# Sine features of k for two of eight batches, made by GpSimd in four forms of instruction

## The chip, the cores and the metric

The kernel runs on one core of one Trainium2 chip. The metric is the device time of the whole program in microseconds. A core has TensorE (PE, matmuls), VectorE (DVE), ScalarE (ACT), GpSimd (POOL) and SyncE (SP, which here only issues DMAs). Each engine takes its instructions in the order in which the program lists them and waits where an operand is not ready.

## The reference

q, k and v have 8 batches of 8 heads, 576 positions and 64 dimensions, in float32. The first half is a linear attention with position weights, the second a gated two-layer network over its output.

```python
theta = np.pi / 2.0 * pos / S
phi(x) = concat([relu(x) * cos(theta), relu(x) * sin(theta)])     # 64 -> 128 features
kv  = einsum('bhsf,bhsd->bhfd', phi(k), v);   z = phi(k).sum(over s)
num = einsum('bhsf,bhfd->bhsd', phi(q), kv)
den = einsum('bhsf,bhf->bhs', phi(q), z) + 1e-6
x   = (num / den), as 4608 rows of 512
h   = x @ w_in                                                   # 512 -> 2048
out = (h * cos(h)) @ w_out                                       # 2048 -> 512
```

Both cosine and sine are positive on the positions used, so relu(x) times the weight equals relu of the product.

## The kernel before

**Tiles.** A batch is laid out as five tiles t = 0 to 4 of 128 rows: each partition holds 4 or 5 positions, and which partitions hold five alternates between even and odd batches. Raw k, q and v come by DMA into one float32 buffer each (tiles km, qm, vm; two DMAs per batch and tensor, L427 and L430). There is one buffer per tensor, so the load of the next batch's k waits until the last feature of this batch's k has been read.

**Features.** `prep` (L443) makes one feature of one tile: 128 partitions by 8 heads by 64 values, g = 0 for cosine and g = 1 for sine, so ten steps per batch for k and ten for q. The weight is a scalar per partition (`CS[:, b % 2, g, t:t+1]`). ACT does it in one activation (Relu with a scale, L452), DVE in one tensor_scalar (maximum with 0, then the product, L453). The result goes as float16 into `kp` or `qp`, both parts of the tile KQ, in blocks of 64 values that lie 128 apart. `cast_v` (L457) casts v to float16, on DVE, ACT or GpSimd (L466 to L468).

**Users.** `kv` (L471) multiplies all k features of a batch with v on TensorE (L479) into the PSUM bank ATT. It needs all ten features and all casts of v. q features are transposed by DMA on the SP queue (`q_dma`, L520), `num` (L542) multiplies them with kv, DVE divides (L568), x is transposed by DMA on SP (`x_dma`, L599) and goes to the two layers: layer 1 in L677 (plain) and L780 (a scheme with seven products of halves, for which DVE makes sums XS of x at L738 and WS of w_in at L717), the gate cos(h) * h by ACT (L609, L802) and DVE (L614, L808), layer 2 in L948 with sums at L926 and L979. TensorE works at layer 1 of one batch and layer 2 of the batch before while the attention of the next batch is prepared.

**What sets the order.** Nothing runs in the order in which the source lists it. Every step is entered in a planner (`Plan`, L129) with its engine or its possible engines, a cost for each, what it reads and writes, and a position in the list KEYS. `Plan.forward` (L183) is a list scheduler: it keeps a clock for each engine, and gives the next step by the smallest key among those that are ready within a small patience. Where a step has several engines, the one that would finish first takes it. Steps marked `port` on DVE and GpSimd are not planned at the same time. Loads become available at their key less 8 us. The program then lists the steps by planned start, which fixes each engine's queue. `either` (L410) enters a step with a choice of engines: cost on DVE is 0.42 us and on ACT 0.62 us for one feature.

In the planner's order for this kernel the ten sine features of k of batches 4 and 5 stand on these engines: batch 4, t = 0 and 2 on DVE and t = 1, 3 and 4 on ACT; batch 5, t = 1 and 3 on DVE and t = 0, 2 and 4 on ACT.

Of the kernel before, what the change touches and what calls it, by code (L numbers as in the profile page):

```python
# [11 lines left out]
ALU = mybir.AluOpType  # L12
# [280 lines left out]
def kernel(  # L293
# [9 lines left out]
    nc = tc.nc  # L303
    B, H, S, D = q.shape
    Dm, Dff = moe_w_in.shape
    P = 128
# [24 lines left out]
    pool = ctx.enter_context(tc.tile_pool(name="pool", bufs=1))  # L331
# [3 lines left out]
    def sb(name, shape, dt=F16):  # L335
        return pool.tile(shape, dt, name=name)
# [73 lines left out]
    def either(due, cost, fn, rd, wr):  # L410

        lat = {"DVE": 0.13, "ACT": 0.15, "POOL": 0.15}
        pl.add([(e, cost[e], cost[e] + lat[e], fn[e]) for e in cost], 0, 0, due, None, rd, wr, port=True)
# [25 lines left out]
    def hk(nm, hs=range(H)):  # L439
        return [((nm, h), n) for h in hs for n in range(2)]  # L440


    def prep(b, nm, t, g, eng, due, hs=slice(0, H), after=()):  # L443
        dst = (kp if nm == "k" else qp)
        out_, in_ = dst[:, t, hs, g, :], raw[nm][:, hs, t, :]
        sc = CS[:, b % 2, g, t:t + 1]
        heads = range(H)[hs]
        rd = hk(nm, heads) + ["CS", *after]
        wr = [(nm + "p", t, g, h) for h in heads]
        f = len(heads) / H  # L450
        cost = {"DVE": 0.09 + 0.33 * f, "ACT": 0.12 + 0.5 * f}
        fn = {"ACT": lambda: nc.scalar.activation(out=out_, in_=in_, func=AF.Relu, scale=sc),  # L452
              "DVE": lambda: nc.vector.tensor_scalar(  # L453
                  out=out_, in0=in_, scalar1=0.0, scalar2=sc, op0=ALU.max, op1=ALU.mult)}
        either(due, {e: c for e, c in cost.items() if eng in (e, "")}, fn, rd, wr)

    def cast_v(b, t, eng, due, hs=slice(0, H), nt=1):  # L457
# [233 lines left out]
    for g in WS:  # L691
        if g < OWN:
            t = sb(f"WS{g}", [P, 3, CH2, GW])
            WS[g].update({n: t[:, n - 2] for n in (2, 3, 4)})
        else:
            for n in (2, 3, 4):
                t = qT[n // 4].rearrange("p h s -> p (h s)").rearrange("p (i c f) -> p i c f", i=2, c=CH2)
# [367 lines left out]
    def first_attention():  # L1065
        for i, nm in enumerate("qkv"):
            dve(0.53, i - 9, lambda nm=nm: nc.vector.memset(raw[nm][:, :, NT, :], 0.0), [],
                [((nm, h), 0) for h in range(H)])
        warm(14, 6.5)
        for nm in ORDER0:  # L1070
            load(0, nm, 0, HALVES if nm == ORDER0[2] else (slice(0, H),))
        weights()
        for t in range(NT):
            prep(0, "q", t, 0, "DVE", t)
            prep(0, "q", t, 1, "DVE" if t == 1 else "ACT", t)
            q_pe(0, t, *BANKS[t], "ACT" if t % 2 else "DVE", t)
        warm(16, 3.45, rd=[("TR", 0)])
        for t in range(NT + 1):
            prep(0, "k", t, 0, "DVE", 4)
            prep(0, "k", t, 1, "DVE" if t == 2 else "ACT", 4)  # L1080
        for hb in range(2):
            for t in range(NT + 1):
                cast_v(0, t, "ACT" if t % 2 else "DVE", 5 + hb, HALVES[hb])
        kv(0, 7, BANKS2)
        for t in range(NT):
            num(0, t, 8 + t, PAIRS0[t % 2])
            if FILL[t]:
                warm(FILL[t], 0.2157 * FILL[t], M1[1],
                     [(("ATT", "M2")[t % 2], 1)], [("M1", 1), ("fill", t)])
            x_pe(0, t, t, *BANKS[3 - t % 2], "ACT", 8 + t, [("fill", t)])  # L1090
# [108 lines left out]
```

## Time and profile before

| what | value |
|---|---|
| median of the runs shown | 285.25 us (283.92 and 286.57) |
| the profiled execution's own time | 284.34 us |
| its span, first to last instruction | 282.3 us |
| granted TensorE clock | 0.993 |
| PE, DVE, ACT, POOL busy | 270.5, 249.2, 218.0, 19.2 us |
| DVE features of k (L453) | 25, mean 482 ns |
| ACT features of k (L452) | 55, median 712 ns |
| GpSimd casts of v, 128x1024 | 9, mean 1088 ns |
| features of k of batch 4 | 91.3 to 104.5 us |
| matmuls of k and v of batch 4, of batch 5 | 108.4, 132.7 us |

The page gives busy time of each engine; the chain of work that ended last follows the releases back from the last instruction; the groups give, for a line and an operation, the output and input tiles, the shapes, the count, the busy time in us, the mean of one in ns, and the idle time of the engine before them with what ended it. In the time order, each line is the start in us, the length in us, the engine, the line, the operation and the tiles, and "xcount" where several neighbours are merged; idle time of the engine before it stands in brackets with its releaser. SPq lines are the issue of a DMA on SP's queue, not its transfer.

### The profile page before, as it was taken

The numbers are of one execution on the slowest core, as the hardware profiler recorded it, in microseconds if no ns is written. First come the engines' busy times: TensorE is split into PE (matmuls) and PEld (weight loads), VectorE is DVE, ScalarE is ACT, GpSimd is POOL, SyncE is SP. The second block draws the span as 40 slices with busy tenths as digits, with TensorE's granted clock in tenths as the row PEclk, the third lists the DMA queues.
The fourth block names the chain that finished last, engine by engine and source line by source line (L and its number), as shares of the span: only waits on it lengthen the run. The fifth ranks groups of instructions, "written<-read, shape, count | busy, mean of one in ns | idle before, by whom it ended". The sixth has DMA issues, their size and how long they took to land.

```text
span 282.3 us, 6870 instructions
## 1 busy us (share of the span) xinstructions
PE 270.5 (96%) x2715; PEld 219.1 (78%) x2715; DVE 249.2 (88%) x443; ACT 218.0 (77%) x396; POOL 19.2 (7%) x32
## 2 busy tenths in 40 slices
PE   7799988999989999999999999999999999999994
PEld 2668956678967667779787988898788888888883
DVE  2877796999999989998999999999999999997952
ACT  2856698896899998599899999996676675877420
POOL 1440020010000010003003000210000000000000
PEclk9799999999999999999999999999999999999999
DMA  6999999969979999997999899988013100300124
GB/s 204 312 200 222 298 291 267 320 133 285 311 231 235 211 229 293 241 310 161 308 234 268 167 275 270 240 117 251 3 37 116 57 2 0 151 0 2 74 77 149
DMA packets 77599, 53.30 MB, mean 189 GB/s; under 512 B 46080, under 2 KB 75264, under 8 KB 77568
## 3 DMA queue, kind: packets, MB, share of 16 engines
q1 hardware_dynamic: 72608, 48.12, 66.7%
q0 software_dynamic: 4224, 4.19, 9.5%
q10 hardware_dynamic: 736, 0.57, 0.6%
q8 instruction: 21, 0.34, 0.5%
q14 instruction: 10, 0.08, 0.1%
HBM read 36.74 MB, written 9.44 MB: 164 GB/s over the span
## 4 chain that ended last, share of the span: by engine, by line
PE 85%; DVE 5%; DMA 4%; ACT 3%; issue 1%; DVEq 0%
PE M L948 32%; PE M L780 15%; PE M L637 10%; PE M L677 7%; PE TR L780 6%; PE M L880 5%; PE ATT L542 3%; DMA xT<-x 2%; PE ATT L479 2%; DMA qm<-in_q_dram 2%; PE M L509 2%; PE ATT L1022 1%; PE TR L677 1%; DVE x L568 1%; ACT xT L593 1%; ACT KQ L452 1%
## 5 line engine op out<-in xcount | busy, mean ns | idle before, releaser
L609 ACT ACTIVATE ch<-M 128x512 f32<-128x512 f32 x90 | 53.3, 597 | 14.4 <-PE M L637 6.9
L614 DVE TENSOR_TENSOR gT<-M,ch 128x512 f16<-128x512 f32 x84 | 56.7, 685 | 5.0 <-ACT ch L609 4.6
L948 PEld LDWEIGHTS <-gT 128*128 128x128 f16 x560 | 54.0, 98 | 7.6 <-DVE gT L926 0.5
L948 PE MATMUL M<-w_out_sb,gT 128*128 128x256 f16 x448 | 55.9, 273 | 0.0
L452 ACT ACTIVATE KQ<-km,CS 128x512 f16<-128x512 f32 x55 | 37.2, 715 | 0.2 <-DMA km<-in_k_dram 0.2
L452 ACT ACTIVATE KQ<-qm,CS 128x512 f16<-128x512 f32 x47 | 32.3, 721 | 4.5 <-DMA qm<-in_q_dram 4.5
L780 PEld LDWEIGHTS <-w_in_sb 128*128 128x128 f16 x320 | 30.8, 98 | 4.3 <-issue 0.2
L948 PE MATMUL M<-T,S 128*128 128x256 f16 x256 | 32.4, 273 | 0.0
L637 PE MATMUL M<-xT,w_in_sb 128*128 128x256 f16 x256 | 30.2, 273 | 0.1
L677 PE MATMUL M<-xT,w_in_sb 128*128 128x512 f16 x112 | 27.6, 379 | 0.8 <-ACT xT L593 0.8
L948 PEld LDWEIGHTS <-S 128*128 128x128 f16 x256 | 24.7, 98 | 4.0 <-issue 0.2
L637 PEld LDWEIGHTS <-w_in_sb 128*128 128x128 f16 x256 | 24.5, 98 | 3.5 <-issue 0.4
L568 DVE TENSOR_TENSOR x<-ATT,rec 128x512 f16<-128x512 f32 x32 | 22.1, 692 | 2.3
L959 ACT ACTIVATE ost<-M 128x512 f32<-128x512 f32 x24 | 14.1, 593 | 12.1 <-PE M L948 9.3
L780 PEld LDWEIGHTS <-WS 128*128 128x128 f16 x216 | 20.5, 98 | 3.3 <-issue 0.5
L677 PEld LDWEIGHTS <-w_in_sb 128*128 128x128 f16 x128 | 12.2, 98 | 10.8 <-issue 0.9
L453 DVE TENSOR_SCALAR KQ<-qm,CS 128x512 f16<-128x512 f32 x33 | 15.4, 498 | 5.1 <-DMA qm<-in_q_dram 5.1
L468 POOL CAST V<-vm 128x1024 f16<-128x1024 f32 (+1 forms) x11 | 10.7, 1004 | 134.9 <-PE M L948 46.0
L542 PEld LDWEIGHTS <-qT 128*128 128x128 f16 x320 | 15.3, 98 | 4.6 <-issue 1.8
L926 DVE TENSOR_TENSOR S<-gT 128x2048 f16<-128x2048 f16 (+1 forms) x16 | 17.4, 1085 | 0.2
L808 DVE TENSOR_TENSOR gT<-Z,ch 128x1024 f16<-128x1024 f32 x13 | 15.9, 1221 | 0.7 <-ACT ch L802 0.4
L542 PE MATMUL ATT<-kvz,qT 128*128 128x65 f16 x288 | 15.7, 194 | 0.6 <-DVE x L568 0.5
(135 smaller groups left out, 461.3 us busy)
## 6 DMA issues: line engine op xcount, KB each, us to landing
out_dram<-ost SPq DMA_DIRECT2D x33, 256.0 KB, 3.0
qm<-in_q_dram SPq DMA_DIRECT2D x8, 640.0 KB, 5.9
km<-in_k_dram SPq DMA_DIRECT2D x8, 640.0 KB, 5.6
qm<-in_q_dram SPq DMA_DIRECT2D x8, 512.0 KB, 6.2
km<-in_k_dram SPq DMA_DIRECT2D x8, 512.0 KB, 5.7
vm<-in_v_dram SPq DMA_DIRECT2D x6, 640.0 KB, 7.2
vm<-in_v_dram SPq DMA_DIRECT2D x6, 512.0 KB, 6.5
w_in_sb<-in_moe_w_in_dram POOLq DMA_DIRECT2D x4, 512.0 KB, 8.9
```

What stands on the lines that cost most here:

```text
L452: fn = {"ACT": lambda: nc.scalar.activation(out=out_, in_=in_, func=AF.Relu, scale=sc), "DVE": lambda: nc.vector.tensor_scalar(out=out_, i ...
L453: "DVE": lambda: nc.vector.tensor_scalar(out=out_, in0=in_, scalar1=0.0, scalar2=sc, op0=ALU.max, op1=ALU.mult)}
L542: nc.tensor.matmul(bank[hb][:, hh * D1:(hh + 1) * D1], lhsT=a[:, h, :], rhs=z[:, h, :], start=(i == 0), stop=(i == len(parts) - 1))
L568: nc.vector.tensor_tensor(out=split(x16[n][:, hs, :], k), in0=A[:, :, :, 0:D], in1=split(rec[n][:, hs], k).unsqueeze(3).broadcast_to((P, k ...
L609: act(0.5, due, lambda: nc.scalar.activation(out=ch[c], in_=bank, func=AF.Sin, bias=math.pi / 2.0, scale=1.0), [key], [("ch", c)])
L614: dve(0.61, due, lambda: nc.vector.tensor_tensor(out=dst, in0=a, in1=b, op=ALU.mult), [key, ("ch", c), *rd], dkeys)
L637: nc.tensor.matmul(M1[m][:, jj * 2 * P:(jj + 1) * 2 * P], lhsT=w_in_sb[:, cc, j * P:(j + 1) * P], rhs=X[:, cc, ts], start=(cc == 0), stop= ...
L677: nc.tensor.matmul(M, lhsT=w_in_sb[:, cc, j * P:(j + 1) * P], rhs=X[:, cc, :], start=(cc == 0), stop=(cc == NCT - 1))
L780: nc.tensor.matmul(bank[0][:, j * TH:(j + 1) * TH], lhsT=a(cc, j), rhs=b[:, cc, :], start=(first and j == 0 and cc == 0), stop=(last and j ...
L808: dve(1.14, due, lambda: nc.vector.tensor_tensor(out=g4, in0=four(uz), in1=four(cc2), op=ALU.mult), zk + ck, [("g", gi(c), h * JH + j, t) ...
L926: dve(0.07 + 1.07 / NG, due, lambda: nc.vector.tensor_tensor(out=out_[:, sl], in0=a[:, sl], in1=b[:, sl], op=op), rd, wr, port=True)
L948: nc.tensor.matmul(bank[0][:, tt * MH:(tt + 1) * MH], lhsT=a[:, j, tt * P:(tt + 1) * P], rhs=b[:, j, :], start=(first and (apart or tt == ...
```

## The change

The five sine features of k (g = 1) of batches 4 and 5 get GpSimd as their only engine. The planner is told 1.2 us for t = 0 to 3 and 2.0 us for t = 4. The forms differ by t: for t = 0 and 1 one tensor_scalar, maximum with 0 and then the product with the weight; for t = 2 one tensor_scalar with the two in the other order; for t = 3 a two-input product with the weight broadcast along the row, and then a tensor_scalar in place for the maximum; for t = 4 a tensor_scalar for the product, and then one in place for the maximum. The values computed are the same. No other step is edited; KEYS is unchanged, and the planner makes its order anew with the new costs and engines.

```diff
@@ -452,6 +452,21 @@
         fn = {"ACT": lambda: nc.scalar.activation(out=out_, in_=in_, func=AF.Relu, scale=sc),
               "DVE": lambda: nc.vector.tensor_scalar(
                   out=out_, in0=in_, scalar1=0.0, scalar2=sc, op0=ALU.max, op1=ALU.mult)}
+        if b in (4, 5) and nm == "k" and g == 1:
+            def pool():
+                q = nc.gpsimd
+                if t < 2:
+                    q.tensor_scalar(out=out_, in0=in_, scalar1=0.0, scalar2=sc, op0=ALU.max, op1=ALU.mult)
+                elif t == 2:
+                    q.tensor_scalar(out=out_, in0=in_, scalar1=sc, scalar2=0.0, op0=ALU.mult, op1=ALU.max)
+                elif t == 3:
+                    q.tensor_tensor(out=out_, in0=in_, in1=sc.unsqueeze(2).broadcast_to((P, H, D)), op=ALU.mult)
+                    q.tensor_scalar(out=out_, in0=out_, scalar1=0.0, scalar2=None, op0=ALU.max)
+                else:
+                    q.tensor_scalar(out=out_, in0=in_, scalar1=sc, scalar2=None, op0=ALU.mult)
+                    q.tensor_scalar(out=out_, in0=out_, scalar1=0.0, scalar2=None, op0=ALU.max)
+            cost, fn = {"POOL": 1.2 if t < 4 else 2.0}, {"POOL": pool}
+            eng = ""
         either(due, {e: c for e, c in cost.items() if eng in (e, "")}, fn, rd, wr)
```

## The prediction

> **What bounds the kernel now.** I read the busy shares first, then the chain that ended last, then the time order from 85 to 135 us, where batches 4 and 5 are prepared.
>
> ```profile
> span 282.3 us, 6870 instructions
> PE 270.5 (96%) x2715; PEld 219.1 (78%) x2715; DVE 249.2 (88%) x443; ACT 218.0 (77%) x396; POOL 19.2 (7%) x32
> PE 85%; DVE 5%; DMA 4%; ACT 3%; issue 1%; DVEq 0%
> ```
>
> TensorE works 96% of the span and holds 85% of the chain; GpSimd is nearly empty. By stretches, PE is busy 13.10 of 13.10 us between 91.3 and 104.4, and 10.70 of 10.70 between 117.7 and 128.4, the two windows in which k of batches 4 and 5 becomes features. Its idle time from 85 to 135 us is two entries: 0.30 us until DVE's XS at L738, and 0.53 us until DVE's x at L568. So relieving ACT or DVE here can give back at most about 0.83 us, 0.3% of the run. A loss has no such limit, because PE takes its instructions in order.
>
> The time order shows how much room there is:
>
> ```profile
> 91.29 1.32 ACT L452 ACTIVATE KQ<-km,CS 128x512 f16<-128x512 f32 x2
> ...
> 103.80 0.71 ACT L452 ACTIVATE KQ<-km,CS 128x512 f16<-128x512 f32 x1
> 104.45 2.05 POOL L468 CAST V<-vm 128x1024 f16<-128x1024 f32 x2 [46.02 <-PE M L948]
> 104.54 0.76 SPq L427 DMA_DIRECT2D km<-in_k_dram  x1
> 108.39 1.37 PE L479 MATMUL ATT<-V,KQ 128*128 128x65 f16 x40
> ...
> 128.40 2.25 POOL L468 CAST V<-vm 128x1024 f16<-128x1024 f32 x2 [21.89 <-DMA vm<-in_v_dram]
> 132.67 1.37 PE L479 MATMUL ATT<-V,KQ 128*128 128x65 f16 x40
> ```
>
> k of batch 4 is read from 91.29 on. Its last feature ends at 104.51; the two casts of v end at 106.50; the matmuls that use both (L479) start at 108.39. Batch 5: the second half of its k load is issued at 111.99 and lands about 5.7 us later (the median of k loads), so at 117.7; casts at 128.40; matmuls at 132.67. The next k load (SP, 104.54) was issued right after the last feature, since raw k has one buffer.
>
> **The change, part by part.** *Removed.* Per batch, five of the ten features. By the planner's order for the kernel before, the ten steps concerned stand as six on ACT and four on DVE. On ACT two of them back to back take 1.32 us, so one is 0.61 us of the queue: 6 x 0.61 = 3.7 us. On DVE one takes 0.48 us and the next instruction starts 0.40 us after it (92.09 to 92.49): 4 x 0.40 = 1.6 us. All of it lies beside a PE without idle time, so I count the gain as nothing; 0.83 us is its upper end.
>
> *Added.* Seven GpSimd instructions per batch: one each for t = 0, 1 and 2 (two operations, one input), two for t = 3 (a two-input product, then an in-place maximum), two for t = 4 (a product, then an in-place maximum). No row shows one of them. The nearest rows are casts:
>
> ```profile
> L468 POOL CAST V<-vm 128x1024 f16<-128x1024 f32 x9 | 9.7, 1088 | 134.9 <-PE M L948 46.0 <-DMA vm<-in_v_dram 40.6 <-PE M L677 26.9
> L468 POOL CAST V<-vm 128x512 f16<-128x512 f32 x2 | 1.2, 625 | 0.0
> L1052 POOL CAST qm<-w_in_sb 2x1 f32<-2x1 f16 x1 | 0.2, 176 | 0.0
> ```
>
> 512 elements cost 0.625 us; almost none cost 0.18. One pass over 512 is therefore 0.45 us. Lower end: every instruction costs one pass, 7 x 0.625 = 4.4 us, plus 0.3 us twice for an in-place instruction that waits for the one before it (the row for that is the 0.31 us between GpSimd's hold at 10.89 and its first load): 5.0 us. I take one pass per operation or input: 0.18 + 2 x 0.45 = 1.07 us for t = 0, 1, 2 and for the product of t = 3, and 0.625 for the three one-operation forms. That is 4 x 1.07 + 3 x 0.625 + 0.6 = 6.8 us, a mean of 0.97 us over seven. It is nearest to the cast row, which is the only GpSimd arithmetic on tiles of this size. Upper end: four passes each, 0.18 + 4 x 0.45 = 1.97 us, 13.8 + 0.6 = 14.4 us. Nothing in the trace excludes still more.
>
> The Trainium skill, page "GPSIMD Engine Reference", section 3.1, gives 4497 ns for a two-input add of 2048 elements and 769 ns for 512 elements in a good one-input loop. By it I estimate six instructions at 0.77 and one at 1.12 us, 5.7 us a batch, which would change nothing below.
>
> *Where it lies.* With 6.8 us, the sines of batch 4 end at 91.3 + 6.8 = 98.1 and those of batch 5 at 117.7 + 6.8 = 124.5. The casts of v stand behind them in GpSimd's queue and start at 104.45 and 128.40 as now. No other GpSimd work, and no DMA from its queue, stands between 60 us and the end except these casts, so nothing else is queued behind the new instructions. The next k load waits for them on SP, with q and x transposes queued behind it; at 98.1 they are earlier than the cosine features on ACT (103.80 now). So the new work is covered: PE above it never waits.
>
> *Contention.* While GpSimd casts, some DVE instructions are longer:
>
> ```profile
> 106.03 0.74 DVE L738 TENSOR_TENSOR XS<-xT 128x512 f16<-128x512 f16 x1 [0.80 <-DMA xT<-x]
> 107.03 0.41 DVE L738 TENSOR_TENSOR XS<-xT 128x512 f16<-128x512 f16 x1
> 129.05 0.68 DVE L453 TENSOR_SCALAR KQ<-qm,CS 128x512 f16<-128x512 f32 x1
> ```
>
> The first two are the same operation: 0.74 us beside the cast that ends at 106.50, 0.41 us without one. The third is 0.68 where 0.48 is usual. DVE pays 0.2 to 0.3 us, and such an instruction can at worst wait for a whole GpSimd one, 1.07 us. The gates (L614), with one operand in PSUM, show nothing of it. In the two windows, each 6.8 us long, I count four exposed DVE instructions that stay: a w_in sum (93.55) and a feature of q (97.11) near batch 4, a cosine feature (119.77) and the 1.22 us gate at L808 (120.16) near batch 5. At 0.5 us each, about half of the worst wait, that is 2.0 us of delay against 1.6 us of removed DVE work: 0.4 us, from -1.6 (none is met) to +2.7 (all wait 1.07). The Trainium skill, page "SBUF — State Buffer", section "Who interferes with whom", states an exclusive lock: the second of the two engines blocks fully until the first is done, for DVE instructions with two SBUF inputs or in a two-port mode. It speaks against this change. The 0.74 us agrees: 106.50 plus about 0.3 is where that instruction ended.
>
> *Order.* The order is made anew by the list planner from the step of batch 4 on, with unchanged keys. I count nothing for it in the sum and keep it as a rival.
>
> Sum: 0 for PE, +0.4 for contention, so 284.34 + 0.4 = 284.7 us. 284.34 is the profiled execution's own time, 0.9 below the median of the two runs, 285.25; the run-to-run distance of 2.65 us is why about 2% (5.7 us) is what a measurement tells from no change. Set against the median as much as against the one execution, I say 285.0, its own range 282.5 to 289.
>
> **The rivals.** *Slow GpSimd (slower).* One mechanism: these forms take m us each on average, and L479 waits for the casts behind them. Batch 4 loses 91.3 + 7m + 2.15 - 108.4 = 7m - 14.95 us, batch 5 117.7 + 7m + 2.35 - 132.7 = 7m - 12.65, if positive. At 2 us that is 1.4 us in all; at 2.4 us 6.0 us, which is where it passes 2%; at 3 us 14.4, so 299; at 4 us 28.4, so 313. SP adds to it: the k load at 104.54 and the transposes behind it are held to 91.3 + 7m. For it: no row shows GpSimd with a per-partition scalar, two operations, or a strided fp16 output in place. Against: the cast is within a third of DVE's and ACT's rows, and 2.4 us would be five passes. The same page of the Trainium skill, section 3.1, names about 12 cycles per element for branching loops. By that, as an estimate, 5.1 us each: the formula then gives 44 us and 328.
>
> *Order of transfers (mostly slower).* With features done earlier, the planner can put the next k load ahead of transposes of x on SP. The chain shows what hangs there:
>
> ```profile
> 99.36 6.57 DMA xT<-x
> 106.03 0.74 DVE XS L738
> ```
>
> A 640 KB load at the 250 GB/s of these stretches is 2.6 us; once per batch it makes XS late by up to 5.2 us, and PE had no slack there (0.30 us idle at L780). That is 285 to 290.5.
>
> *Faster.* To pass 2% the new order would have to remove 5.7 us of the PE idle time of 11.8 us, of which 8.2 lie in the first 20 and the last 62 us. 278.5 at best.
>
> That the change does nothing can't be: GpSimd is the only engine left in the options of these steps.
>
> **How the numbers follow.** Covered: 0.48. Slow GpSimd: 0.32, all beyond 2%. Order: 0.16, of which 0.06 within 2% and 0.10 slower. Faster: 0.04. So faster 0.04, same 0.54, slower 0.42. The range leaves out about 0.08 below 282.5 and about 0.12 above 300 (slow GpSimd beyond 3.05 us each).
>
> **What would show it.** Covered: POOL rows at the new lines behind L453 near 0.6 to 1.1 us, their last start before 104 and 128 us, no idle time at L479. Slow GpSimd: a mean above 2.4 us, casts of v later than 106 and 130, and PE waiting for POOL at L479 or SP waiting for POOL before a k load. Contention: DVE instructions of L453, L717 and L808 above 0.5, 0.42 and 1.23 us. Order: PE waiting at L780 for XS, with a DMA piece for xT longer than 6.57 us in the chain. The prediction fails first if the middle value for two operations is wrong, since it alone decides whether the cover holds.

## The result and the profile after

The changed kernel takes 329.99 us (median of two runs, 329.53 and 330.45) against 285.25 us before: a ratio of 1.157, with a 95% interval from 1.133 to 1.181. The forecast was 285.0 us; its range, with the rivals counted in, went from 282.5 to 300. The time lies far outside it. One run among those below, 329.57 us of the new order without GpSimd, was in a slower state of the chip; the median given for that kernel counts it, the ratio does not, and that kernel's profile is of this run.

The head of the page of the changed kernel:

```profile
span 328.7 us, 6868 instructions
PE 284.2 (86%) x2715; PEld 220.9 (67%) x2715; DVE 261.2 (79%) x446; ACT 216.7 (66%) x386; POOL 41.9 (13%) x43
PEclk9999999999999999899897999979999999999998
```

PE does the same 2715 matmuls, but its idle time is 328.7 - 284.2 = 44.5 us, where it was 11.8: +32.7 us. Its busy time is 13.7 us longer too; the row of the granted clock (a slice is 8.2 us) now has sevens and eights from about 131 us on, where before it had none after its second slice.

The new instructions, by shape (groups on GpSimd, changed kernel; after the bar: busy us, mean ns of one, idle before):

```profile
L459 POOL TENSOR_SCALAR KQ<-km,CS 128x512 f16<-128x512 f32 x4 | 8.3, 2070 | 32.2 <-PE ATT L557 32.2
L461 POOL TENSOR_SCALAR KQ<-km,CS 128x512 f16<-128x512 f32 x2 | 4.0, 2006 | 15.2 <-DMA km<-in_k_dram 15.2
L464 POOL TENSOR_SCALAR KQ<-KQ 128x512 f16<-128x512 f16 x2 | 3.9, 1935 | 0.2
L466 POOL TENSOR_SCALAR KQ<-km,CS 128x512 f16<-128x512 f32 x2 | 3.8, 1898 | 0.0
L467 POOL TENSOR_SCALAR KQ<-KQ 128x512 f16<-128x512 f16 x2 | 3.0, 1512 | 0.2
L463 POOL TENSOR_TENSOR KQ<-km,CS 128x512 f16<-128x512 f32 x2 | 2.1, 1040 | 0.0
```

They are slower than the 0.97 us that I took on average, but not the 2.4 us at which a slow GpSimd was to cost 2%. In the order of time they end as follows, with the casts of v behind them (GpSimd, changed kernel; start us, length us):

```profile
91.03 2.00 POOL L459 TENSOR_SCALAR KQ<-km,CS 128x512 f16<-128x512 f32 x1 [32.16 <-PE ATT L557]
...
100.79 2.00 POOL L459 TENSOR_SCALAR KQ<-km,CS 128x512 f16<-128x512 f32 x1
104.90 2.06 POOL L483 CAST V<-vm 128x1024 f16<-128x1024 f32 x2 [2.12 <-DVE gT L629]
122.13 2.02 POOL L461 TENSOR_SCALAR KQ<-km,CS 128x512 f16<-128x512 f32 x1 [15.17 <-DMA km<-in_k_dram]
...
134.18 1.53 POOL L467 TENSOR_SCALAR KQ<-KQ 128x512 f16<-128x512 f16 x1
135.67 1.05 POOL L483 CAST V<-vm 128x1024 f16<-128x1024 f32 x1
```

Batch 4 takes from 91.0 to 102.8, 11.8 us, and the casts start at 104.90, not 104.45. Batch 5 takes 13.6 us, from 122.1 to 135.7. It begins later than the 117.7 us of the forecast because the second half of its k load stands later in SP's new order (issued at 116.08, before at 111.99). All but the first two of PE's matmuls of k and v of batch 5 then start at 136.8, 4.1 us later than before. Up to 137 us PE has had 5.4 us more idle time than before; the other 27 of its 33 us of new idle time come afterwards, where GpSimd does nothing new.

PE's waits say what for (list of waits of PE, changed kernel: waiting line, releaser, us in total, times, longest):

```profile
PE M L795 <- ACT M L678: 5.0, 7, 1.3
PE ATT L557 <- DVE x L583: 4.2, 3, 2.1
PE M L795 <- DVE gT L629: 3.5, 4, 1.4
...
PE M L963 <- DVE gT L629: 2.7, 2, 1.9
PE TR L795 <- DVE Z L808: 2.3, 2, 1.5
PE M L795 <- ACT Z L804: 1.9, 3, 0.9
...
PE ATT L494 <- POOL V L483: 0.3, 1, 0.3
```

Only 0.3 us of PE's waiting names a cast that stands behind GpSimd's features. Most of the rest, 26 us, are waits inside the two layers, and 19 us of these stand at the products of the fast scheme of layer 1 (L795, formerly L780), which wait for the copies and gates between them. At L780 PE waited 0.3 us before. How this begins can be seen in PE's order of time, changed kernel:

```profile
124.95 1.04 PE L963 MATMUL M<-w_out_sb,gT 128*128 128x256 f16 x8
125.91 1.91 PE L963 MATMUL M<-T,gT 128*128 128x256 f16 x16
127.66 1.04 PE L963 MATMUL M<-w_out_sb,gT 128*128 128x256 f16 x8
130.07 0.60 PE L795 MATMUL M<-xT,w_in_sb 128*128 128x256 f16 x4 [1.38 <-DVE gT L629]
131.34 0.60 PE L795 MATMUL M<-xT,w_in_sb 128*128 128x256 f16 x4 [0.67 <-ACT M L678]
```

and in the same place before:

```profile
125.68 0.60 PE L780 MATMUL TR<-XS,WS 128*128 128x256 f16 x4
126.12 0.60 PE L780 MATMUL M<-xT,w_in_sb 128*128 128x256 f16 x4
126.56 1.04 PE L948 MATMUL M<-w_out_sb,gT 128*128 128x256 f16 x8
127.43 0.60 PE L780 MATMUL M<-xT,w_in_sb 128*128 128x256 f16 x4
```

Before, layer-2 products (L948) stand between the short, mutually dependent products of layer 1 and fill the time in which ACT and DVE work on their banks. Now four such layer-2 products stand in a row, and the layer-1 products that follow have nothing between them. By stretches, PE spent 8.85 us on layer 2 between 120 and 140 us before, and 4.78 now, after 10.92 (9.87 before) between 100 and 120.

### The profile page after: what moved, and what is told of

Read it like the earlier page. It is cut to its first block, busy times and chain, and to the rows that moved or that the text cites. A ratio compares the mean times of both kernels' runs of the same rounds, so it can differ in the third digit from the quotient of the medians.

```text
span 328.7 us, 6868 instructions
## 1 busy us (share of the span) xinstructions
PE 284.2 (86%) x2715; PEld 220.9 (67%) x2715; DVE 261.2 (79%) x446; ACT 216.7 (66%) x386; POOL 41.9 (13%) x43
## 5 line engine op out<-in xcount | busy, mean ns | idle before, releaser
L963 PEld LDWEIGHTS <-gT 128*128 128x128 f16 x560 | 54.7, 99 | 14.9 <-DVE gT L629 3.3
L963 PE MATMUL M<-w_out_sb,gT 128*128 128x256 f16 x448 | 57.4, 278 | 4.5 <-DVE gT L629 2.7
L795 PEld LDWEIGHTS <-w_in_sb 128*128 128x128 f16 x320 | 32.0, 101 | 17.8 <-issue 13.0
L452 ACT ACTIVATE KQ<-qm,CS 128x512 f16<-128x512 f32 x50 | 33.5, 713 | 4.7 <-DMA qm<-in_q_dram 4.5
L652 PE MATMUL M<-xT,w_in_sb 128*128 128x256 f16 x256 | 30.2, 272 | 0.5 <-DVE gT L629 0.3
L795 PEld LDWEIGHTS <-WS 128*128 128x128 f16 x216 | 21.2, 100 | 11.3 <-issue 7.6
L452 ACT ACTIVATE KQ<-km,CS 128x512 f16<-128x512 f32 x41 | 27.2, 715 | 0.6 <-DMA km<-in_k_dram 0.5
L652 PEld LDWEIGHTS <-w_in_sb 128*128 128x128 f16 x256 | 24.4, 98 | 4.0 <-issue 1.1
L974 ACT ACTIVATE ost<-M 128x512 f32<-128x512 f32 x24 | 14.3, 596 | 19.4 <-PE M L963 14.4
L692 PEld LDWEIGHTS <-w_in_sb 128*128 128x128 f16 x128 | 12.1, 97 | 12.5 <-issue 3.0
L808 DVE TENSOR_TENSOR Z<-M,Z 128x512 f32<-128x512 f32 x22 | 14.9, 688 | 6.8 <-PE M L795 6.0
L817 ACT ACTIVATE ch<-Z 128x1024 f32<-128x1024 f32 x14 | 14.7, 1053 | 7.2 <-DVE Z L808 7.2
L795 PE MATMUL M<-xT,w_in_sb 128*128 128x256 f16 x96 | 14.8, 278 | 4.3 <-ACT M L678 2.4
```

Source lines behind the costliest of these rows:

```text
L652: nc.tensor.matmul(M1[m][:, jj * 2 * P:(jj + 1) * 2 * P], lhsT=w_in_sb[:, cc, j * P:(j + 1) * P], rhs=X[:, cc, ts], start=(cc == 0), stop= ...
L692: nc.tensor.matmul(M, lhsT=w_in_sb[:, cc, j * P:(j + 1) * P], rhs=X[:, cc, :], start=(cc == 0), stop=(cc == NCT - 1))
L795: nc.tensor.matmul(bank[0][:, j * TH:(j + 1) * TH], lhsT=a(cc, j), rhs=b[:, cc, :], start=(first and j == 0 and cc == 0), stop=(last and j ...
L808: dve(0.61, due + 0.3, lambda: nc.vector.tensor_tensor(out=dst, in0=bank[0], in1=dst, op=ALU.add), [bank[1], key], [key])
L817: act(0.86, due, lambda: nc.scalar.activation(out=cc2, in_=uz, func=AF.Sin, bias=math.pi / 2.0, scale=1.0), zk, ck)
L963: nc.tensor.matmul(bank[0][:, tt * MH:(tt + 1) * MH], lhsT=a[:, j, tt * P:(tt + 1) * P], rhs=b[:, j, :], start=(first and (apart or tt == ...
```

## The experiments

(The planner's class begins at L126, not at the L129 given for it above.) Two theories: the new order made by the planner costs the time (1), or GpSimd's slow instructions and what they block do (2). The line numbers of a changed kernel are shifted by the lines put in.

**The old order, with the sines on GpSimd.** The planner sees the costs of before; only the instruction that a step writes is exchanged.

```diff
-            cost, fn = {"POOL": 1.2 if t < 4 else 2.0}, {"POOL": pool}
-            eng = ""
+            fn = {"ACT": pool, "DVE": pool}
```

> The planner is given the costs and engines of before, so every engine's queue is that of before; only the ten sine steps are then written as the GpSimd instructions of the change. PE's and SP's queues are those of before, instruction by instruction. Theory 1 (the new order is what costs): 284 to 287 us. From the trace of the changed kernel the seven instructions take 11.8 us for batch 4 and 13.5 us for batch 5; by the prediction's formula batch 4 then loses nothing and batch 5 117.7 + 13.5 + 2.35 - 132.7 = 0.9 us, so 285.2 on a profile of 284.3. Theory 2 (slow GpSimd instructions and what they block are what costs): at least half of the 45 us stays, above 307 us.

Measured: 284.98 us, ratio 0.998 (0.994 to 1.002). The same ten sines, in the same four forms, cost nothing. The head of its page and its GpSimd rows near batch 5:

```profile
PE 270.7 (95%) x2715; PEld 219.0 (77%) x2715; DVE 251.0 (88%) x439; ACT 214.9 (76%) x390; POOL 43.1 (15%) x46
```

```profile
117.87 2.00 POOL L461 TENSOR_SCALAR KQ<-km,CS 128x512 f16<-128x512 f32 x1 [10.21 <-DMA km<-in_k_dram]
...
128.52 1.49 POOL L467 TENSOR_SCALAR KQ<-KQ 128x512 f16<-128x512 f16 x1
129.96 2.24 POOL L482 CAST V<-vm 128x1024 f16<-128x1024 f32 x2
```

PE is busy for 270.7 us, as before. GpSimd has the five sines of batch 5 done 12.1 us after it begins, and the cast of v follows 1.6 us later than before. Theory 2, by which at least half of the loss would stay, falls.

**The new order, without GpSimd.** The planner plans as in the changed kernel; the ten steps are then written as the ACT and DVE instructions of before.

```diff
-            cost, fn = {"POOL": 1.2 if t < 4 else 2.0}, {"POOL": pool}
+            old = fn["DVE" if (b, t) in ((4, 0), (4, 2), (5, 1), (5, 3)) else "ACT"]
+            cost, fn = {"POOL": 1.2 if t < 4 else 2.0}, {"POOL": old}
```

> The planner plans as in the changed kernel, as if the ten steps stood on GpSimd; they are then written as the ACT and DVE instructions that they were before (six on ACT, four on DVE). PE's and SP's queues are those of the changed kernel, instruction by instruction; GpSimd does none of the features. Theory 1 (order): 325 to 335 us, as the changed kernel. Theory 2 (GpSimd): near 285 to 290 us. If both share, something between.

Measured: 327.06 us, ratio 1.140 (1.132 to 1.149). The loss stays when GpSimd does none of the features. PE, whose queue is that of the changed kernel, waits at the same place for the same gate and copy, and reaches the matmuls of k and v of batch 5 no earlier:

```profile
130.83 0.60 PE L796 MATMUL M<-xT,w_in_sb 128*128 128x256 f16 x4 [1.64 <-DVE gT L630]
132.91 1.01 PE L796 MATMUL M<-xT,w_in_sb 128*128 128x256 f16 x4 [1.48 <-ACT M L679]
...
138.05 1.37 PE L495 MATMUL ATT<-V,KQ 128*128 128x65 f16 x40
```

The two runs together are theory 1 from both sides: the old queues of PE and SP with GpSimd give the old time, the new queues without GpSimd give 41.1 of the 44.7 us. Whether GpSimd has a part in the other 3.6 us is open: the interval of this ratio overlaps that of the change, 1.133 to 1.181.

**One cost, 0.01 us more.** The kernel before, no instruction exchanged; the planner is told 0.43 and 0.63 us in place of 0.42 and 0.62 for one single step.

```diff
+        if (b, nm, t, g) == (4, "k", 0, 1):
+            cost = {e: c + 0.01 for e, c in cost.items()}
```

> The kernel before, with one number changed: the cost that the planner is told for one sine step (batch 4, k, t = 0) is 0.01 us higher on ACT and DVE. No instruction changes its engine or form by an edit, and GpSimd gets nothing; only the order is made anew. Theory 1 (any new order made from these keys costs): the planner's own last step moves by 38 us, as it does in the changed kernel, so 310 to 335 us. Theory 2 (GpSimd): 285 us. A rival within theory 1, that the planner's order is harmless and its large effect comes from planning the GpSimd steps too long or too short: 285 to 290 us.

Measured: 324.20 us, ratio 1.134 (1.128 to 1.139). PE's waits are of the same kind as in the changed kernel:

```profile
PE M L782 <- ACT Z L791: 6.0, 4, 2.3
PE M L782 <- ACT M L665: 4.1, 7, 0.9
```

So the loss needs neither GpSimd nor a freed engine; 0.01 us on one planned cost is enough. In the plan it moves the steps behind it on DVE, from 91.4 us on, by 0.01 us. Near 95.3 us a feature then takes the place of a gate in DVE's queue, and from 97 us on PE's queue differs too.

**The same, on another step (t = 1).**

> As the run with 0.01 us more on the planned cost of batch 4, k, sine, t = 0, but on t = 1. The planner's own last step then moves by 23 us and not by 38. Theory (the time follows the planned order): 302 to 315 us, below the 324.2 of the step t = 0. Rival (a new order costs about 40 us whatever it is): 320 to 330 us.

Measured: 308.07 us, ratio 1.082 (1.076 to 1.089). The loss belongs to the particular order and is not a fixed price. These two steps are the only ones on which the 0.01 us was tried.

**The change, with keys that name the old order.** KEYS are replaced by the starts that the planner gave before; the ten steps are planned and made on GpSimd as in the change.

```diff
-KEYS = (
-    5824, 5995, 5824, 2967, 2673, 126, 143, -359, -2881, 263, -1072, -2121, 539, -49, 2962,
...
+KEYS = (
+    0, 106, 53, 0, 0, 71, 136, 201, 266, 331, 396, 461, 940, 990, 1170, 1080, 1260, 1642, 1672,
...
```

> The changed kernel with its ten steps on GpSimd, planned there at the same costs, but KEYS replaced by the starts that the planner gave in the kernel before, in hundredths of a us: the priorities then say the old order directly. The planner's last step stands 2 us behind that of before. Theory 1 (order): 285 to 291 us. Theory 2 (GpSimd): above 307 us.

Measured: 288.63 us, ratio 1.010 (1.005 to 1.016). 42 of the 45 us are gone, with the change itself in place. Its control has the same keys and no GpSimd:

> The kernel before, features on ACT and DVE as before, with KEYS replaced by the starts that the planner gave: the control of the run that had these keys with ten steps on GpSimd (288.6 us). The planner's last step stands 2 us behind that of before. If those 3 us over before were the order: 286 to 290 us. If they were GpSimd: 284 to 286 us.

Measured: 287.31 us, ratio 1.010 (1.007 to 1.013). The two ratios agree within their intervals. So the remaining 1% goes with the order that these keys give, and GpSimd's part in it is too small to be measured here.

**Every sine twice on GpSimd, in the old order.** This tests the price that the prediction gave to a slow GpSimd. The edit is shown against the first experiment.

```diff
-            fn = {"ACT": pool, "DVE": pool}
+            def twice():
+                pool()
+                pool()
+            fn = {"ACT": twice, "DVE": twice}
```

> The order of before, with every sine step of batches 4 and 5 written twice on GpSimd (the second pass computes the same values again). PE's and SP's queues are those of before. It tests the price that the prediction gave to a slow GpSimd, apart from any new order. From the run in the old order with one pass the instructions take 11.8 us (from 91.0) for batch 4 and 12.1 us (from 117.9) for batch 5; twice that is 23.6 and 24.2 us. Theory 1 (the matmuls of k and v wait for the casts of v behind the features, as the formula says): batch 4 loses 91.0 + 23.6 + 2.15 - 108.4 = 8.4 us, batch 5 117.9 + 24.2 + 2.35 - 132.7 = 11.8 us, so about 304 us. Rival (SP, which holds the next k load and the transposes behind it, comes first and adds its own): 308 to 320 us. Rival (the slack is larger than the formula says): below 295 us.

Measured: 309.31 us, ratio 1.086 (1.079 to 1.092). PE, at the matmuls of k and v:

```profile
116.37 0.27 PE L496 MATMUL ATT<-V,KQ 128*128 128x65 f16 x2 [8.01 <-POOL V L485]
117.36 2.25 PE L496 MATMUL ATT<-V,KQ 128*128 128x65 f16 x38 [0.72 <-POOL V L485]
154.07 0.27 PE L496 MATMUL ATT<-V,KQ 128*128 128x65 f16 x2 [10.64 <-POOL V L485]
155.06 2.25 PE L496 MATMUL ATT<-V,KQ 128*128 128x65 f16 x38 [0.72 <-POOL V L485]
```

The waits are 8.7 and 11.4 us, where the formula gave 8.4 and 11.8; their sum, 20.1, is the 20.2 that was expected. The loss is 24.8 us. PE's busy time is 275.3 us, 4.8 more than before, which is the size of the difference. The time of 309 lies in the range that the SP rival had, but not for its reason: SP did hold the next k load for 10.8 us, yet among PE's waits these four are the only new ones of any size, and none names a load or a transpose. The formula's term was right, and what it lacked is the slower PE behind a wait (the last section).

The planner runs without the chip. Its own clock, put beside the chip's, for all orders (last end of a step in the plan, and how many of PE's 440 steps, each some matmuls, changed their place in the queue against before; the last column is against the kernel before, measured together with it):

| kernel | plan's end, us | PE steps moved, farthest | measured, us | measured less before of the same runs |
|---|---|---|---|---|
| before | 278.5 | 0 | 285.25 | 0 |
| old order, GpSimd | 278.5 | 0 | 284.98 | -1.0 |
| control of the keys | 280.6 | 58, by 5 | 287.31 | +2.8 |
| change, rekeyed | 280.8 | 53, by 5 | 288.63 | +2.7 |
| cost + 0.01, t = 1 | 301.4 | 247, by 27 | 308.07 | +23.5 |
| the change | 316.5 | 288, by 34 | 329.99 | +44.7 |
| the change's order, no GpSimd | 316.5 | 288, by 34 | 327.06 | +41.1 |
| cost + 0.01, t = 0 | 316.7 | 284, by 32 | 324.20 | +38.2 |

The chip follows the plan within 7 us. Most of the loss, 38 of the 45 us, could be read in the plan before the program reached the chip.

## Why the prediction was wrong

**The step that failed is "Order"**: "I count nothing for it in the sum and keep it as a rival." The term was put at nothing without a reason, and it was nearly the whole loss: the new order alone, without GpSimd, costs 41 of the 45 us. The rival under that name was mis-sized, 285 to 290.5 for the order of transfers on SP, and had the wrong place: no wait of PE in the changed kernel names a load, only 1.0 us names a transpose, and the sign that it had named, PE waiting for XS, is not there. What moved was PE's own queue, in 288 of 440 steps. I looked at the 50 us around the ten steps and priced what could happen there; the list planner makes every later choice anew, and the 190 us behind that stretch hold most of the loss.

That the order is brittle could have been seen without the chip: the planner itself puts its last end at 316.5 us where it was 278.5. The code shows why. KEYS are some 1400 numbers without a visible rule, and steps are given by the smallest key among those that are ready. Such keys fix a good order only together with the times at which steps get ready. Shift one such time by 0.01 us, and another step can be ready first, as the run with one cost shows.

**PE bounds the kernel, a gain is at most 0.83 us**: held. In the old order ten features less on ACT and DVE gave 0.998, no difference. ACT's busy time fell by 3.1 us (the forecast had 3.7). DVE's did not fall by 1.6 but rose by 1.7, since other instructions of DVE became longer (see Contention).

**The price of the instructions**: too low. The sum was 6.8 us a batch, between 5.0 and 14.4; measured are 11.8 and 12.1 in the old order. One pass per operation was wrong for tensor_scalar: two operations cost 2.00 us where I took 1.07, one costs 1.5 where I took 0.63. For the two-input product the 1.07 was right (1.04). From the Trainium skill, page "GPSIMD Engine Reference", section 3.1, I had estimates of 1.12 us for the two-input form, which the 1.04 us agrees with, and of 0.77 us for a one-input form, which the 1.5 us does not bear out. The prediction had said that the value for two operations alone decides whether the cover holds. It was half of what was measured, and the cover held all the same, as 11.8 us is under the 14.95 at which batch 4 would have begun to pay, and 12.1 under the 12.65 of batch 5.

**Slow GpSimd as a rival**: the mechanism was right and its formula good to half a us, as the doubled run shows, but these instructions do not reach its threshold. That the measured 330 lies next to a 328 of the prediction is chance. The 328 came from 5.1 us each, an estimate from a figure of the Trainium skill, page "GPSIMD Engine Reference", section 3.1; none of the new instructions of the changed kernel took over 2.34 us.

**Contention**: present, and small for the kernel. In the old order the sum XS at L752 takes 0.94 us beside a cast (0.41 alone), the sum of w_in right behind it 1.26 (0.41 before), and a feature of q at 129.93 us 1.36 (0.68 before). That is more per instruction than the 0.2 to 0.3 us read in the rows of before, and goes with DVE's busy time not falling. PE waits 1.0 us for XS where it waited 0.3. The kernel's time does not show it.

What is not settled: which of the exchanged steps cost the time, and why the change loses 6.5 us more than the order of cost + 0.01, t = 0, with nearly the same planned end. For the first, the plan only shows where the two orders part: PE's queue is the same up to steps planned at 96 us. No run here isolates one exchange.

## What to carry to other kernels

Where a program writes its own order from a list of tuned priorities, an edit to one step's cost or engine is an edit to the whole order behind it, and that comes first in the sum. Run the planner first and compare its last end with the old one: here it moved by 38 us. Before judging an engine or an instruction form in such a kernel, hold the order fixed and exchange only the instruction; then change the order by itself. When the engine that bounds the kernel has no idle time to give back, what is left of such a change is the risk of its order.

## What the runs showed of the hardware

A tensor_scalar on GpSimd is slower than a two-input product there: 1.5 us for one operation and 2.0 us for two, on 128x512, against 1.04 us. The order of the two operations makes no difference (2.00 us at L459, and at L461 too, where nothing delayed it), and a per-partition scalar is not what makes it slow, since the in-place maximum with plain constants takes 1.49 us as well. What the reason is, no run here shows. Some of the same instructions take longer: one with one operation 2.34 us in the changed kernel (at 127.40, beside DVE's gate L823, which takes 2.01 us where 1.22 is usual), and two with two operations 3.06 us in the rekeyed kernel. These two begin at 88.17 and 116.76 us, each within 0.1 us of a DVE sum of 1.22 us with two SBUF operands (L990, L937). In the old order such a sum (L993 at 118.76) stands beside a sine, and neither is longer. What decides it was not tested.

Behind some waits PE's matmuls are slower for a time. In the changed kernel the granted clock is 0.88 between 137 and 165 us, where the clock before was 1.00 at every stretch from 20 us to 220; there, behind waits of 1.05 and 1.47 us, sixteen matmuls of layer 2 take 3.37 us where 1.91 is usual. Idle time alone does not do it: between 120 and 137 us the changed kernel's PE is idle for 4.5 us, and the clock is 1.00. With every sine doubled, stretches with waits of 8.7 and 11.4 us have 0.76 and 0.75:

```profile
104.50:119.00 14.50, 5.18 (x54) 3.64 (x52) 8.50 (x13) 4.57 (x9) 12.43 (x9) 0.76 0.35 54
119.00:133.00 14.00, 14.00 (x133) 11.35 (x131) 9.40 (x17) 8.54 (x17) 5.55 (x3) 0.88 1.11 258
133.00:160.00 27.00, 15.63 (x152) 13.15 (x150) 12.42 (x22) 11.71 (x21) 21.25 (x14) 0.75 0.57 162
```

```profile
119.42 3.36 PE L965 MATMUL M<-w_out_sb,gT 128*128 128x256 f16 x16
```

The columns of the first three lines are the stretch, its length, busy us with instructions of PE, PEld, DVE, ACT and POOL, the granted clock, the DMA share and GB/s. The stretch from 119 to 133 us has no idle PE time and still 0.88; its first sixteen matmuls of layer 2, the last line, take 3.36 us where 1.91 is usual. Taken together, the matmuls right behind the two waits take about 5 us more than usual, and PE's busy time grew by 4.8 us. Slower matmuls of this kind are a part of the 13.7 us by which PE's busy time grew in the changed kernel; how large a part was not measured.
